# Turning x to token rows on VectorE and by copies inside the memory instead of on TensorE (attention and token mixing, one core)

## The chip, the cores and the metric

The kernel runs on one core of one Trainium2 chip. The metric is the device time of one execution in microseconds (us). A core has TensorE (PE, with its weight loads PEld), VectorE (DVE), ScalarE (ACT), GpSimd (POOL) and SyncE (SP), which here does nothing but issue DMAs. Each engine takes its instructions in the order in which the program lists them, and waits on semaphores for the others.

## The reference

Eight batches of attention (8 heads, 576 tokens, head size 64) with two kinds of masks, then a mixing block on the 512 channels that the heads make up together:

```
x = attention(q, k, v)                  # per batch: 576 tokens x 512 channels
theta = x @ w_theta
zr, zi = x * cos(theta), x * sin(theta)
y = w_tok_r @ zr + w_tok_i @ zi         # over the tokens
u = x + y
out = u + relu(u @ w_ch)
```

## The kernel before, in words

**Layout.** The attention of a batch b goes in four pairs of heads. `pv` leaves the pair's output in PSUM, `x_evac` copies it to the tile `x{pr}` in the memory: 128 rows are channels, 576 columns are tokens. theta, the residual and the channel product use x in this form (channels on the rows). The products `x * sin` and `x * cos` need the other form, tokens on the rows, since `theta` leaves theta with 128 tokens on the rows and 512 channels along them.

**Turning x.** `natural(b, st)` makes that other form for a tile `st` of 128 tokens (st 4 is the last half tile of 64): four TensorE transposes (L718) of 128 x 128 into one PSUM bank `xn`. VectorE then multiplies out of PSUM: L760 (sin, into `g`) and L702 (cos, into `K`) for tiles 0 to 3, L767 and L702 for tile 4.

**One batch's stages.** `phase(b, nb)` lists what TensorE does, and PE's order is that of the code. First come the eight *token units* `y` of batch b (L804; 27 matmuls each, over nine K tiles in the order `KORD` = 0, 4, 1, 5, 2, 6, 3, 7, 8), with the scores `s` and the products `o` of the next batches between them. The scores of pair 2 of batch b+1 stand ahead of the first token unit of batch b. Then comes the *theta stage*: theta of tile 4, 0, 1, 2, 3 of batch nb (`th`, L682 to L689), each followed by a channel unit `c` of batch b (L834, 12 matmuls) and, before the change, by the transposes of `natural`. The last three channel units end the phase.

**From theta to z.** `trig(b, st)` is a chain over ACT and DVE. ACT copies theta to an integer (`K`, L746), DVE subtracts it (L748), ACT takes the sine into `g` (L754), the absolute value (L695) and the cosine (L697), DVE multiplies both with x. `zsplit` then rounds each product on ACT (`zh{kt}`, L641) and takes the rest on POOL (`zl{kt}`, L643). Token tile st gives the K tiles st (cosine) and 4 + st (sine); tile 4 gives K tile 8. A token unit reads all of them.

**What else stands on DVE, ACT and POOL near there.** L813 takes a channel unit out of its PSUM bank (`c`, two banks `m`). The scores of a pair are masked and their row maximum taken by nine instruction pairs (L406), L495 scales the maximum, nine ACT exponentials with sums follow (L501, with a table load ahead of them after sines), DVE takes the reciprocal of the sums (L504, L505), POOL multiplies (`P`, L507), and DVE turns P by eight block transposes of 32 rows each (L522).

**What sets the order.** For the first phase (batch 0, and theta of batch 1) the order on DVE, ACT, POOL and SP comes from `Order`, a list scheduler with ranks and costs in the code. From then on only PE's order is written down; the order on the other engines is set at build time by the framework's scheduler, which simulates the program. The eight completion semaphores of SP's DMAs are used in turn, so a DMA waits until the eighth before it has landed.

Of the kernel before, what the change touches and what calls it, by code (L numbers as in the profile page):

```python
# [18 lines left out]
DM = H * D  # L19
# [40 lines left out]
class Order:  # L60
# [13 lines left out]
    def pin(self, ins):  # L74
        if self.live:
            self.tc.keep_in_program_order(ins)
# [73 lines left out]
def build(ctx, tc, qT, kT, vw, wth, wtk, wch, maskb, ident, identb, outT):  # L150
# [431 lines left out]
    def x_split(b, pr):  # L582
        yield None, ("xe", b, pr)
        x = xf[b, pr]
        yield from take(f"xh{pr}", 1, XH.get(pr) if b == 1 else None)
        hl = hp.tile([128, 2 * S], F32R, tag=f"xh{pr}", name=f"xh{b}_{pr}")
        hi = hl[:, :S]
        lo, lt = hl[:, S + 64:], hl[:, S:S + 64]
        yield "ACT", act(S)
        pin(nc.scalar.copy(hi, x))  # L590
        on = pr < 3
        eng, cost = (nc.vector, dve) if on else (nc.gpsimd, pool)
        yield "DVE" if on else "POOL", cost(64)
        pin(eng.tensor_tensor(lt, x[:, FS:], hi[:, FS:].bitcast(F32), op=ALU.subtract))
        yield "DVE" if on else "POOL", cost(FS)
        pin(eng.tensor_tensor(lo, x[:, :FS], hi[:, :FS].bitcast(F32), op=ALU.subtract))
        xh[b, pr] = hl
        signal(("xh", b, pr))

    def pv(b, pr):  # L600
        yield None, ("va", b, pr)
        yield None, ("vb", b, pr)
        yield None, ("pt", b, pr)
        if pr >= 1:
            yield None, ("pv", b, pr - 1)
# [12 lines left out]
        n = b * NP + pr  # L618
        if ra is not None:
            give("va", ra)  # L620
            go(load_va(n + 2), RANK["load"])
        if rb is not None:
            give("vb", rb)
            go(load_vb(NP if n == NP - 2 else n + 1), RANK["load"])
        if b:
            go(x_split(b, pr))

    zs = {}

# [63 lines left out]
    def cosine(b, st, f, z, kt, key, rel):  # L693
        yield "ACT", act(DM)
        pin(nc.scalar.activation(f, f, AF.Abs))  # L695
        yield "ACT", act(DM) + 90
        table(nc.scalar.activation(f, f, AF.Sin, scale=-2 * math.pi, bias=halfpi[:f.shape[0]]))  # L697
        signal(("sin", b, st))
        yield None, ("xn", b, st)
        px, rx = pxs[b, st]  # L700
        yield "DVE", dve(DM)
        pin(nc.vector.tensor_tensor(z, px, f, op=ALU.mult))  # L702
        signal(key)
        if kt is not None:
            yield None, ("px", b, st)
            give(*rx)
            yield from zsplit(b, kt, z, rel)
        elif rel:
            give(*rel)

    pxs = {}

    def natural(b, st, cs):
        px, rx = yield from bank("mmxxm"[st] if b == 0 else "x" if b == 1 else XP[st], f"xn{b}_{st}")
        px = px[:cs.stop - cs.start]
        yield "PE", 430
        for c in range(NC):
            pe(nc.tensor.transpose(px[:, 128 * c:128 * c + 128], xf[b, c][:, cs], idt))  # L718
        pxs[b, st] = px, rx
        signal(("xn", b, st))  # L720

    def trig(b, st):
        cs = slice(128 * st, min(128 * st + 128, S))
        R = cs.stop - cs.start
        yield None, ("th", b, st) if b else ("th0", st, 3)
        pt, rt = ths.pop((b, st))
        go(natural(b, st, cs))
        if b == 0 and st in FG0:
            K, gt = (hp.tile([128, DM], F32R, tag=t, name=f"{n}{b}_{st}").bitcast(F32) for t, n in zip(FG0[st], "Kg"))
            K = K.bitcast(I32)[:R]  # L730
            rf = rg = None
        else:
            rf, rg = ("f", (yield from take("f", 2))), ("g", (yield from take("g", 2)))
            K = gp.tile([128, DM], I32, tag="f", name=f"K{b}_{st}")[:R]
            gt = gp.tile([128, DM], F32, tag="g", name=f"g{b}_{st}")
        f = K.bitcast(F32)
        g = gt[:R]
        th = pt[:R]
        if R == 64 and b > 0:
            yield "ACT", act(DM)  # L740
            pin(nc.scalar.copy(g, pt[R:]))
            yield "DVE", dve(DM)
            pin(nc.vector.tensor_tensor(g, th, g, op=ALU.add))
            th = g
        yield "ACT", act(DM)
        pin(nc.scalar.activation(K, th, AF.Copy, scale=I2PI))  # L746
        yield "DVE", dve(DM)
        pin(nc.vector.scalar_tensor_tensor(out=f, in0=th, scalar=I2PI, in1=K, op0=ALU.mult, op1=ALU.subtract))  # L748
        give(*rt)
        if b == 0:  # L750
            for p in range(NP):
                yield None, ("P", 0, p)
        yield "ACT", act(DM)
        table(nc.scalar.activation(g, f, AF.Sin, scale=2 * math.pi))  # L754
        if R == 128:
            go(cosine(b, st, f, f, st, ("cos", b, st), rf))
            yield None, ("xn", b, st)
            px, rx = pxs[b, st]
            yield "DVE", dve(DM)
            pin(nc.vector.tensor_tensor(g, px, g, op=ALU.mult))  # L760
            signal(("px", b, st))
            yield from zsplit(b, 4 + st, g, rg)
        else:
            yield None, ("xn", b, st)
            px, rx = pxs[b, st]
            yield "DVE", dve(DM)
            pin(nc.vector.tensor_tensor(gt[128 - R:], px, g, op=ALU.mult))  # L767
            yield from cosine(b, st, f, g, None, ("cos", b, st), rf)
            give(*rx)
            yield from zsplit(b, 8, gt, rg)  # L770

    uh, ul = {}, {}
# [68 lines left out]
    def phase(b, nb):  # L841
        if nb >= B:
            for f, i, g in UNITS:
                go(f(b, i, g))
            return
        n = 0
        while n <= TH_AT:
            for p in S_AT:
                if S_AT[p] == n and nb + p // NP < B:
                    go(scores(nb + p // NP, p % NP))  # L850
            f, i, g = UNITS[n]
            go(f(b, i, g))
            for p in range(NP):
                if PV_AT[p] == n:
                    go(pv(nb, p))
            for p in TURN_AT:
                if TURN_AT[p] == n and nb + p // NP < B:
                    go(turn(nb + p // NP, p % NP))
            n += 1
        rest = UNITS[n:]  # L860
        for i, st in enumerate(STS):
            go(theta(nb, st))
            f, e, g = rest.pop(0)
            go(f(b, e, g))
            go(trig(nb, st))
            for p in TURN_TH:
                if TURN_TH[p] == i and nb + p // NP < B:
                    go(turn(nb + p // NP, p % NP))
        while rest:
            f, i, g = rest.pop(0)  # L870
            go(f(b, i, g))
# [55 lines left out]
    for p in range(2):  # L927
        go(scores(2, p), RANK["scores2"] + p * RANK["pair"])
        go(turn(2, p), RANK["scores2"] + p * RANK["pair"])
    go(thetas(1), RANK["theta1"])  # L930
    od.run()
    od.live = False
# [70 lines left out]
```

## Time and profile before

| | us |
|---|---|
| median of 3 runs (597.99 to 598.87) | 598.78 |
| the profiled execution's own time | 597.07 |
| its span (first to last instruction) | 595.3 |

| engine | busy us | share of the span |
|---|---|---|
| PE | 569.7 | 96% |
| DVE | 361.6 | 61% |
| ACT | 351.1 | 59% |
| POOL | 222.4 | 37% |

The phases of the batches in the middle repeat at a distance of 68.7 us. In what follows one of them is read, with times in us from the start of the span: the theta stage of batch 4 lies from 319.7 to 348.3, and the first token unit of batch 4 starts at 349.5.

### The profile page before, as it was taken

The numbers are of one execution on the slowest core, as the hardware profiler recorded it, in microseconds if no ns is written. First come the engines' busy times: TensorE is split into PE (matmuls) and PEld (weight loads), VectorE is DVE, ScalarE is ACT, GpSimd is POOL, SyncE is SP. The second block draws the span as 40 slices with busy tenths as digits, with TensorE's granted clock in tenths as the row PEclk, the third lists the DMA queues.
The fourth block names the chain that finished last, engine by engine and source line by source line (L and its number), as shares of the span: only waits on it lengthen the run. The fifth ranks groups of instructions, "written<-read, shape, count | busy, mean of one in ns | idle before, by whom it ended". The sixth has DMA issues, their size and how long they took to land.

```text
span 595.3 us, 14176 instructions
## 1 busy us (share of the span) xinstructions
PE 569.7 (96%) x5584; PEld 516.9 (87%) x5584; DVE 361.6 (61%) x1132; ACT 351.1 (59%) x939; POOL 222.4 (37%) x206
## 2 busy tenths in 40 slices
PE   5997898999999999999999999999999999999997
PEld 4744787979998899889998899989998899989997
DVE  3889888855765667465566567655665656445112
ACT  1498967687535955568553974468564785266110
POOL 2229854534322532326142442316324253315220
PEclk9999599999999999999999999999999999999999
DMA  8982347404650074302641054401742023001002
GB/s 303 398 339 61 121 160 246 142 1 141 182 160 3 2 241 142 101 2 89 197 139 62 1 181 151 154 1 40 231 142 73 0 81 100 1 1 53 28 1 81
DMA packets 26866, 67.76 MB, mean 114 GB/s; under 512 B 2992, under 2 KB 3248, under 8 KB 26800
## 3 DMA queue, kind: packets, MB, share of 16 engines
q1 hardware_dynamic: 26800, 66.86, 32.9%
q8 instruction: 44, 0.72, 0.5%
q14 instruction: 22, 0.18, 0.1%
HBM read 57.41 MB, written 9.44 MB: 112 GB/s over the span
## 4 chain that ended last, share of the span: by engine, by line
PE 49%; DVE 22%; ACT 21%; issue 3%; POOL 2%; DMA 2%; SPq 0%; ACTq 0%; DVEq 0%; POOLq 0%
PE y L804 27%; DVE pt L522 9%; PE c L834 8%; PE s L465 5%; ACT P L501 5%; PE o L614 4%; PE th L682 3%; ACT K L697 3%; ACT zh L641 3%; ACT g L754 2%; ACT K L695 2%; DVE P L406 2%; DVE K L702 2%; POOL P L507 2%; ACT L754 1%
## 5 line engine op out<-in xcount | busy, mean ns | idle before, releaser
L787 POOL TENSOR_TENSOR u<-x,u 128x288 fp32r<-128x288 f32 x64 | 54.9, 858 | 184.9 <-ACT u L785 162.2
L522 DVE STREAM_TRANSPOSE pt<-P 32x288 f32<-32x288 f32 x224 | 105.1, 469 | 21.1 <-POOL P L507 18.0
L834 PE MATMUL c<-u,late_wc 128*128 128x288 f32 x768 | 111.7, 296 | 0.8 <-DVE x L813 0.5
L834 PEld LDWEIGHTS c<-u,late_wc 128*128 128x128 f32 x768 | 106.2, 188 | 4.8 <-DVE x L813 2.0
L785 ACT CAST u<-x 128x288 fp32r<-128x288 f32 x64 | 27.5, 430 | 129.3 <-DVE x L782 129.3
L804 PE MATMUL y<-wtkh,zh 128*128 128x288 f32 x288 | 90.6, 315 | 1.1 <-ACT zh L641 1.1
L804 PE MATMUL y<-wtkh,zl 128*128 128x288 f32 x288 | 86.6, 301 | 3.7 <-POOL zl L643 3.7
L804 PE MATMUL y<-wtkl,zh 128*128 128x288 f32 x288 | 86.2, 299 | 0.0
L643 POOL TENSOR_TENSOR zl<-g,zh 128x512 fp32r<-128x512 f32 x40 | 52.6, 1316 | 79.1 <-ACT zh L641 66.7
L501 ACT ACTIVATE P<-P,mx 128x64 f32<-128x64 f32 x216 | 72.1, 336 | 16.8 <-DVE mx L495 16.8
L682 PE MATMUL th<-wthh,xh 128*128 128x512 f32 x224 | 76.3, 402 | 0.0
L782 DVE TENSOR_TENSOR x<-y,x 128x288 f32<-128x288 f32 x64 | 28.7, 450 | 66.8 <-PE y L804 64.0
L804 PE MATMUL y<-late_wt_b,zh 128*128 128x288 f32 x320 | 68.1, 297 | 0.0
L804 PE MATMUL y<-late_wt_a,zh 128*128 128x288 f32 x256 | 58.0, 308 | 2.7 <-DVE x L782 2.7
L804 PEld LDWEIGHTS y<-wtkh,zh 128*128 128x128 f32 x288 | 55.4, 192 | 4.8 <-ACT zh L641 2.3
L804 PEld LDWEIGHTS y<-wtkh,zl 128*128 128x128 f32 x288 | 55.3, 192 | 4.5 <-POOL zl L643 4.5
L804 PEld LDWEIGHTS y<-wtkl,zh 128*128 128x128 f32 x288 | 55.5, 193 | 0.3 <-issue 0.3
L643 POOL TENSOR_TENSOR zl<-K,zh 128x512 fp32r<-128x512 f32 x32 | 42.0, 1312 | 36.1 <-ACT zh L641 36.1
L507 POOL TENSOR_TENSOR P<-P,sm 128x576 f32<-128x576 f32 x32 | 37.5, 1172 | 43.8 <-ACT xh L590 19.3
L804 PEld LDWEIGHTS y<-late_wt_b,zh 128*128 128x128 f32 x320 | 51.4, 189 | 0.3
L682 PEld LDWEIGHTS th<-wthh,xh 128*128 128x128 f32 x224 | 42.1, 188 | 8.3
L804 PE MATMUL y<-late_wt_b,zl 128*128 128x288 f32 x160 | 47.3, 296 | 0.0
(103 smaller groups left out, 1110.0 us busy)
## 6 DMA issues: line engine op xcount, KB each, us to landing
q<-in_qT_dram SPq DMA_DIRECT2D x32, 576.0 KB, 4.2
va<-in_vw_dram SPq DMA_DIRECT2D x30, 320.0 KB, 3.2
out_dram<-x SPq DMA_DIRECT2D x32, 288.0 KB, 2.1
k<-in_kT_dram SPq DMA_DIRECT2D x28, 304.0 KB, 4.6
vb<-in_vw_dram SPq DMA_DIRECT2D x29, 256.0 KB, 3.4
st_wtk<-in_wtk_dram SPq DMA_DIRECT2D x8, 576.0 KB, 8.8
st_wth<-in_wth_dram SPq DMA_DIRECT2D x4, 512.0 KB, 9.8
st_wch<-in_wch_dram SPq DMA_DIRECT2D x4, 512.0 KB, 4.9
```

The lines of the kernel that those rows point to most:

```text
L465: pe(nc.tensor.matmul(ps[64 * e:64 * e + 64, n - g0], q[:, qb], k[:, QB * qb:QB * qb + BW], start=not masked, stop=not masked or n == g1 - 1))
L501: table(nc.scalar.activation(P[:, n], P[:, n], AF.Exp, bias=mx[:, n:n + 1], scale=SCALE, accum_out=sm[:, n:n + 1]))
L507: pin(nc.gpsimd.tensor_tensor(P, P, sm.unsqueeze(2).to_broadcast([128, NJ, BW]), op=ALU.mult))
L522: pin(nc.vector.transpose(pmats[b, pr][k0:k0 + QB, :, hh, QB * e:QB * e + QB], P[p0:p0 + QB, :, QB * o:QB * o + QB]))
L614: pe(nc.tensor.matmul(ps[64 * hh:64 * hh + 64, BW * j:BW * j + BW], v[:, 64 * hh:64 * hh + 64], pmats[b, pr][:, j, hh], start=True, stop=T ...
L643: pin(nc.gpsimd.tensor_tensor(lo, z, hi.bitcast(F32), op=ALU.subtract))
L682: pe(nc.tensor.matmul(pt, l, r, start=(n == 0), stop=(n == 3 * NC - 1)))
L782: pin(nc.vector.tensor_tensor(x[:, ts], ps, x[:, ts], op=ALU.add))
L785: pin(nc.scalar.copy(uh[b, d][:, ts], x[:, ts]))
L787: pin(nc.gpsimd.tensor_tensor(ul[b, d][:, ts], x[:, ts], uh[b, d][:, ts].bitcast(F32), op=ALU.subtract))
L804: pe(nc.tensor.matmul(ps, l[:, cs], r, start=(n == 0), stop=(n == 3 * NK - 1)))
L834: pe(nc.tensor.matmul(ps, l[:, cs], r[:, ts], start=(n == 0), stop=(n == 3 * NC - 1)))
```

## The change

From batch 1 on `natural` does nothing. In its place:

- `x_turn` (L726 of the changed kernel, called from `pv` behind `x_split`) turns a pair's x on VectorE: one block transpose over 128 rows x 576 columns, which turns each 32 x 32 block in itself, into the tile `xq`. Four for each batch, 28 in all.
- `x_move` (L743, called in `phase` ahead of the theta stage) brings the blocks to their rows by DMAs within the memory: each moves 32 rows x 128 words (512 B a row, 16 KB). 16 for a tile of 128 tokens, 8 for the half tile: 72 for each batch, 504 in all, all on SP. It has no tile of its own to write to: `xn` of token tile st takes the buffer of `zh{4+st}` (that of K tile 8 for the half tile). So these DMAs wait until the token units of the batch before have read that buffer for the last time, and for all four `x_turn`s; and `zh` of that K tile is written only when both products of the tile are done.
- the products (`by_x`, L765) read `xn` from the memory in place of PSUM, with the channel order of `xn` folded into the access pattern.
- `dynamic_dma_scratch_size=1024` makes room in the memory for `xq`.

Batch 0 is turned on TensorE as before.

```diff
         if b:
             go(x_split(b, pr))
+            go(x_turn(b, pr))
...
+    def x_turn(b, c):
+        yield None, ("xe", b, c)
+        if c == 0:
+            yield from take("xq", 1, b - 1)
+            xq[b] = cp.tile([128, 18, NC, QB], F32, tag="xq", name=f"xq{b}")
+        elif od.live:
+            yield None, ("got", "xq", b - 1)
+        yield "DVE", 1000
+        pin(nc.vector.transpose(xq[b][:, :, c], xf[b, c].rearrange("p (a s) -> p a s", s=QB)))
+        signal(("xq", b, c))
+
+    def x_move(b):
+        for c in range(NC):
+            yield None, ("xq", b, c)
+        if b == 1:
+            for d in range(NC):
+                yield None, ("tk", 0, d, 1)
+        for st in STS:
+            R = 64 if st == 4 else 128
+            kt = min(4 + st, 8)
+            xn = hp.tile([128, DM], F32R, tag=f"zh{kt}", name=f"xn{b}_{st}").bitcast(F32)
+            yield "DMA", dma(R // 128 * DM)
+            for a in range(R // QB):
+                for g in range(4):
+                    pin(nc.sync.dma_start(xn[QB * a:QB * a + QB, 128 * g:128 * g + 128],
+                                          xq[b][QB * g:QB * g + QB, 4 * st + a].rearrange("p a b -> p (a b)")))
+            xns[b, st] = xn[:R].rearrange("p (g c d) -> p c g d", g=4, c=NC)
+            signal(("xn", b, st))
+        give("xq", b - 1)
...
     def natural(b, st, cs):
-        px, rx = yield from bank("mmxxm"[st] if b == 0 else "x" if b == 1 else XP[st], f"xn{b}_{st}")
+        if b:
+            return
+        px, rx = yield from bank("mmxxm"[st], f"xn{b}_{st}")
...
+    def by_x(b, st, z, f):
+        if b:
+            pin(nc.vector.tensor_tensor(rows(z), xns[b, st], rows(f), op=ALU.mult))
+        else:
+            pin(nc.vector.tensor_tensor(z, pxs[b, st][0], f, op=ALU.mult))
...
             yield "DVE", dve(DM)
-            pin(nc.vector.tensor_tensor(g, px, g, op=ALU.mult))
+            by_x(b, st, g, g)
             signal(("px", b, st))
+            if b:
+                yield None, ("cos", b, st)
             yield from zsplit(b, 4 + st, g, rg)
...
         rest = UNITS[n:]
+        go(x_move(nb))
         for i, st in enumerate(STS):
             go(theta(nb, st))
...
+    go(x_move(1), 0)
     go(thetas(1), RANK["theta1"])
```

Since the scheduler of the build sets the order on DVE, ACT, POOL and SP, the order moves too. Three places around the end of the theta stage of batch 4 follow. In the names the digits behind the letter are batch and tile: `K4_3` is the cosine side of token tile 3 of batch 4, `g4_3` its sine side, `c3_3_1` the last channel unit of batch 3, `s5_2`, `P5_2`, `mx5_2`, `sm5_2` belong to the scores of pair 2 of batch 5, `y4_0_0` is the first token unit of batch 4.

**DVE, from the last channel units to the first token unit.** Before (the other L406 pairs left out):

```order
L748 SCALAR_TENSOR_TENSOR K4_3_4345<-th4_3_4312,K4_3_4345 128x512
L813 SCALAR_TENSOR_TENSOR x3_1_2844<-c3_1_1_4362,x3_1_2844 128x288
L702 TENSOR_TENSOR K4_3_4345<-xn4_3_4340,K4_3_4345 128x512
L760 TENSOR_TENSOR g4_3_4346<-xn4_3_4340,g4_3_4346 128x512
L813 SCALAR_TENSOR_TENSOR x3_3_3054<-c3_3_1_4392,x3_3_3054 128x288
L406 ISA P5_2_4407,mx5_2_4408<-s5_2_0_4410,mskb_91 128x64
L495 TENSOR_SCALAR mx5_2_4408<-mx5_2_4408 128x9
L782 TENSOR_TENSOR x4_0_3607<-y4_0_0_4456,x4_0_3607 128x288
L504 TENSOR_SCALAR sm5_2_4409<-sm5_2_4409 128x9
```

And in the changed kernel:

```order
L861 SCALAR_TENSOR_TENSOR x3_3_3172<-c3_3_1_4620,x3_3_3172 128x288
L765 TENSOR_TENSOR K4_1_4484<-xn4_1_4316,K4_1_4484 128x512
L765 TENSOR_TENSOR g4_1_4485<-xn4_1_4316,g4_1_4485 128x512
L406 ISA P5_2_4635,mx5_2_4636<-s5_2_0_4638,mskb_91 128x64
L795 SCALAR_TENSOR_TENSOR K4_3_4573<-th4_3_4545,K4_3_4573 128x512
L495 TENSOR_SCALAR mx5_2_4636<-mx5_2_4636 128x9
L504 TENSOR_SCALAR sm5_2_4637<-sm5_2_4637 128x9
L765 TENSOR_TENSOR K4_2_4528<-xn4_2_4333,K4_2_4528 128x512
L765 TENSOR_TENSOR g4_2_4529<-xn4_2_4333,g4_2_4529 128x512
L765 TENSOR_TENSOR K4_3_4573<-xn4_3_4350,K4_3_4573 128x512
L765 TENSOR_TENSOR g4_3_4574<-xn4_3_4350,g4_3_4574 128x512
L830 TENSOR_TENSOR x4_0_3778<-y4_0_0_4684,x4_0_3778 128x288
```

Before, the products of tiles 1 and 2 were long done here and those of tile 3 stood ahead of the last channel unit; now those of tile 1 stand behind the last channel unit, and those of tiles 2 and 3 behind the reciprocal of the sums of the next scores (L504, L505).

**ACT and POOL at the same place.** Before, ACT rounded the last z tiles and then took the exponentials:

```order
L697 ACTIVATE K4_3_4345<-K4_3_4345,halfpi_93 128x512
L641 CAST zh4_3_4353<-K4_3_4345 128x512
L641 CAST zh4_7_4358<-g4_3_4346 128x512
L501 ACT_TABLE_LOAD
L501 ACTIVATE P5_2_4407,sm5_2_4409<-P5_2_4407,mx5_2_4408 128x64 x9
```

Now the exponentials stand ahead of the four last z tiles:

```order
L698 ACTIVATE K4_3_4573<-K4_3_4573,halfpi_93 128x512
L501 ACT_TABLE_LOAD
L501 ACTIVATE P5_2_4635,sm5_2_4637<-P5_2_4635,mx5_2_4636 128x64 x9
L642 CAST zh4_2_4536<-K4_2_4528 128x512
L642 CAST zh4_6_4541<-g4_2_4529 128x512
L642 CAST zh4_3_4581<-K4_3_4573 128x512
L642 CAST zh4_7_4586<-g4_3_4574 128x512
```

POOL follows the same turn: its product for P5_2 (L507) stood behind all nine `zl` of batch 4, and stands now between the `zl` of K tile 5 and those of K tiles 2, 6, 3 and 7.

**SP, from the last loads of the token stage to the next ones.** Before, the outputs of batch 3 followed the loads:

```order
L220 DMA k5_3_4036<-in_kT_dram 128x608
L819 DMA out_0_dram<-x3_0_2726 128x576
L819 DMA out_0_dram<-x3_1_2844 128x576
L819 DMA out_0_dram<-x3_2_2913 128x576
L819 DMA out_0_dram<-x3_3_3054 128x576
L218 DMA q6_0_4439<-in_qT_dram 128x1152
```

In the changed kernel the 72 copies stand between:

```order
L220 DMA k5_3_4212<-in_kT_dram 128x608
L743 DMA xn4_0_4299<-xq4_3807 32x128 x4
L743 DMA xn4_4_4290<-xq4_3807 32x128 x8
L743 DMA xn4_0_4299<-xq4_3807 32x128 x12
L743 DMA xn4_1_4316<-xq4_3807 32x128 x16
L743 DMA xn4_2_4333<-xq4_3807 32x128 x16
L743 DMA xn4_3_4350<-xq4_3807 32x128 x16
L867 DMA out_0_dram<-x3_0_2840 128x576
```

The loads before them are past; the outputs and the next loads of q stand behind them.

More of the change, by code (lines that the diff above doesn't have):

```diff
@@ L699, in cosine @@
         yield None, ("xn", b, st)
-        px, rx = pxs[b, st]
         yield "DVE", dve(DM)
-        pin(nc.vector.tensor_tensor(z, px, f, op=ALU.mult))
+        by_x(b, st, z, f)
         signal(key)
         if kt is not None:
-            yield None, ("px", b, st)
-            give(*rx)
+            if not b:
+                yield None, ("px", b, st)
+                give(*pxs[b, st][1])
             yield from zsplit(b, kt, z, rel)
@@ L711, in build, with rows @@
     pxs = {}
+    xq, xns = {}, {}
+    def x_turn(b, c):
[26 more added lines that the diff above has]
+        give("xq", b - 1)
+    def rows(t):
+        return t.rearrange("p (c g d) -> p c g d", c=NC, g=4)
     def natural(b, st, cs):
-        px, rx = yield from bank("mmxxm"[st] if b == 0 else "x" if b == 1 else XP[st], f"xn{b}_{st}")
+        if b:
+            return
+        px, rx = yield from bank("mmxxm"[st], f"xn{b}_{st}")
         px = px[:cs.stop - cs.start]
@@ L757, in trig @@
             yield None, ("xn", b, st)
-            px, rx = pxs[b, st]
             yield "DVE", dve(DM)
-            pin(nc.vector.tensor_tensor(g, px, g, op=ALU.mult))
+            by_x(b, st, g, g)
             signal(("px", b, st))
+            if b:
+                yield None, ("cos", b, st)
             yield from zsplit(b, 4 + st, g, rg)
@@ L764, in trig @@
             yield None, ("xn", b, st)
-            px, rx = pxs[b, st]
             yield "DVE", dve(DM)
-            pin(nc.vector.tensor_tensor(gt[128 - R:], px, g, op=ALU.mult))
+            by_x(b, st, gt[128 - R:], g)
             yield from cosine(b, st, f, g, None, ("cos", b, st), rf)
-            give(*rx)
+            if not b:
+                give(*pxs[b, st][1])
             yield from zsplit(b, 8, gt, rg)
@@ L989 @@
     host = _arrays({n: _np.asarray(a) for n, a in inputs.items()})
-    nc = _bacc.Bacc("TRN2", target_bir_lowering=False, num_devices=1)
+    nc = _bacc.Bacc("TRN2", target_bir_lowering=False, num_devices=1,
+                     dynamic_dma_scratch_size=1024)
     arrays, args = {}, []
```

## The prediction

> **What bounds the kernel now.** I read the page first, then the busy time by stretches, then PE's waits, and last the timelines of all engines around one theta stage.
>
> ```profile
> span 595.3 us, 14176 instructions
> 276.23:344.89 68.66, 67.90 (x676) 63.06 (x676) 42.69 (x155) 42.19 (x121) 24.34 (x24) 1.00 0.32 106
> PE y L804 <- DVE x L782: 0.5, 1, 0.5
> PE c L834 <- DVE x L813: 0.2, 1, 0.2
> ```
>
> The second line is one period of the middle batches (columns: length, busy us of PE, PEld, DVE, ACT and POOL with instruction counts, PE's granted clock, DMA share, GB/s); the last two are all of PE's waits in it. PE is busy for 67.90 of 68.66 us at full clock and waits twice, 0.7 us in all. It looks like a kernel bound by PE alone, from which any PE work taken away is gain. The theta stage shows how little stands beside that:
>
> ```profile
> 319.74 0.39 PE L687 MATMUL th<-wthh,xh 128*128 128x512 f32 x1
> 323.16 0.60 PE L718 MATMUL xn<-idt,x 128*64 128x128 f32 x4
> 323.52 0.48 PE L682 MATMUL th<-wthh,xh 128*128 128x512 f32 x1
> 342.91 5.44 PE L834 MATMUL c<-u,late_wc 128*128 128x288 f32 x36
> 348.28 1.27 PE L465 MATMUL s<-k,q 128*64 128x64 f32 x36
> 349.48 0.40 PE L804 MATMUL y<-wtkh,zh 128*128 128x288 f32 x1
> ```
>
> Four transposes hold PE from 323.16 to 323.52, 0.36 us. The stage goes from 319.74 to 348.28, scores follow, and the first token unit of batch 4 starts at 349.48. At that time its last inputs are still being made:
>
> ```profile
> 348.08 1.28 POOL L643 TENSOR_TENSOR zl<-K,zh 128x512 fp32r<-128x512 f32 x1 [1.52 <-ACT zh L641]
> 349.32 1.29 POOL L643 TENSOR_TENSOR zl<-g,zh 128x512 fp32r<-128x512 f32 x1
> 353.37 0.46 DVE L782 TENSOR_TENSOR x<-y,x 128x288 f32<-128x288 f32 x1 [2.64 <-DMA q<-in_qT_dram]
> ```
>
> The `zl` of token tile 3 end at 349.3 and 350.6; PE reaches those K tiles (seventh and eighth of nine) some 2.5 and 3 us after 349.48 and never waits. The unit's end, 353.3, is seen in L782. So the z chain has about 2 us to spare there, no more: **whatever puts the products of tiles 2 and 3 later by more than that stops PE at the first token unit of every batch.**
>
> **What is removed.** 20 transposes for each of 7 batches. By the rows above 5 x 0.36 = 1.8 us of PE for a batch, 12.6 in all, at once in front of the token unit. The PSUM banks that come free cost or win nothing here: PE's two waits are on banks `m`.
>
> **What is added, and beside what it lies.**
>
> ```profile
> L522 DVE STREAM_TRANSPOSE pt<-P 32x288 f32<-32x288 f32 x224 | 105.1, 469 | 21.1 <-POOL P L507 18.0
> L760 DVE TENSOR_TENSOR g<-xn,g 128x512 f32<-128x512 f32 x32 | 21.9, 683 | 2.2 <-ACT g L754 1.3 <-PE xn L718 0.8
> L767 DVE TENSOR_TENSOR g<-xn,g 64x512 f32<-64x512 f32 x8 | 5.5, 684 | 8.9 <-ACT g L754 8.8
> 311.66 3.85 DVE L522 STREAM_TRANSPOSE pt<-P 32x288 f32<-32x288 f32 x8 [1.90 <-POOL P L507]
> ```
>
> No transpose of 128 rows is in this trace. The nearest row is L522, 469 ns for 32 rows x 288. Rows cost nothing on DVE (L767 with 64 rows and L760 with 128 take 684 and 683), so twice the columns give 0.94 us; if the four strips of 32 rows went one after another it were 3.75. I take 0.94. Three of the four lie in the token stage, where DVE is half idle (42.69 of 68.66). The fourth, of pair 3, falls into the 1.90 us in which DVE waits for P ahead of 311.66: nothing, but 2.8 us a batch at the upper end. The products read two operands from the memory instead of one from PSUM; their step (0.6, below) I leave as it is.
>
> The copies:
>
> ```profile
> 1.16 0.42 SPq L270 DMA_DIRECT2D idb<-in_identb_dram  x1
> 1.63 0.42 SPq L279 DMA_DIRECT2D q<-in_qT_dram  x1
> 280.93 0.34 SPq L218 DMA_DIRECT2D q<-in_qT_dram  x1
> 281.32 0.45 SPq L220 DMA_DIRECT2D k<-in_kT_dram  x1
> out_dram<-x SPq DMA_DIRECT2D x32, 288.0 KB, 2.1
> ```
>
> SP issues DMAs 0.39 us (280.93 to 281.32) to 0.47 us apart (1.16 to 1.63), whatever their size; a small one lands 2.1 us after. All these move 128 rows and none stays inside the memory. I take 0.39 with the 0.47 as upper row; with eight semaphores the 2.1 us allow one each 0.26 us, so issuing sets the pace. 72 of them take 28 us. All but four wait for the last token unit, which ends at 319.7; tile 1 has then landed by 319.7 + 40 x 0.39 + 2.1 = 337.4, tile 2 by 343.7, tile 3 by 349.9. Behind them in SP's queue are only outputs and a load of q for a much later pair; nobody waits for those. The buffers of `zh` bring no stall either: the casts stand behind both products anyway. The smaller scratch space touches no transfer that this kernel makes.
>
> **What is moved, and where it costs.** DVE's order in the changed kernel now has the products of tiles 2 and 3 behind L504 and L505, thus behind the nine exponentials of the next scores, which stand behind the row maxima, which need PE's scores; and the maxima stand behind the copy-out of the last channel unit and the products of tile 1. The copies may land early, DVE cannot take the products before. The links, by their rows:
>
> ```profile
> 347.26 0.68 DVE L760 TENSOR_TENSOR g<-xn,g 128x512 f32<-128x512 f32 x1
> 347.86 0.99 DVE L813 SCALAR_TENSOR_TENSOR x<-c,x 128x288 f32<-128x288 f32 x2
> 349.13 0.22 DVE L406 CUSTOM_DVE_ANT_0 P<-s,mskb 128x64 f32<-128x64 f32 x1 [0.28 <-PE s L465]
> 350.56 0.17 DVE L495 TENSOR_SCALAR mx<-mx 128x9 f32<-128x9 f32 x1
> 344.57 0.63 ACT L754 ACTIVATE g<-K 128x512 f32<-128x512 f32 x1
> 345.23 0.63 ACT L695 ACTIVATE K<-K 128x512 f32<-128x512 f32 x1
> 345.90 0.73 ACT L697 ACTIVATE K<-K,halfpi 128x512 f32<-128x512 f32 x1
> 348.62 1.28 ACT L501 ACT_TABLE_LOAD   x1
> 317.59 3.09 ACT P L501 x18
> 355.19 1.15 POOL L507 TENSOR_TENSOR P<-P,sm 128x576 f32<-128x576 f32 x1
> ```
>
> I walk them in batch 4's times. PE ends the last channel unit at 348.28 less 1.8 (transposes) less 0.2 (the wait) = 346.3. Copy-out 0.5: 346.8. Two products of tile 1, 0.6 each (347.26 to 347.86): 348.0. Five of nine maxima, 0.16 each (349.13 to 350.56): 348.8. The second half of the scores reuses the bank that these free: 16 of 36 matmuls, 0.6: 349.4. Four maxima: 350.1. The subtraction of tile 3, 0.6: 350.7. Sine, absolute value and cosine on ACT, 0.66 + 0.67 + 0.73: 352.8. Table load 1.28: 354.1. Exponentials 3.09: 357.2. Sum and reciprocal, about 0.4: 357.6. Four products: 360.0. POOL meanwhile makes P, 1.15, to 358.8, then four `zl` at 1.25 (348.08 to 349.32): 363.8. The last four matmuls of the unit: **364.3, against 353.3 now: 11.0 us late**, with PE idle for some 8 of them. From the unit's end to the next theta stage PE is full as before, so nothing takes this back: DVE's work there starts earlier against PE than it did.
>
> Batches 1 to 6 have this order (1 with small differences; there SP starts within the stage, and I hold it at 11.0 too): 66. Batch 7 has no scores behind it: the maxima, exponentials and P fall out of the chain, but tile 1's products still wait for the last channel unit, and from there copy, subtraction, two ACT steps, rounding and four `zl` follow; the same steps give about 7.5. Sum 73.5.
>
> **The clock.** A PE that idles for 8 us does not come back at full speed:
>
> ```profile
> 50.00:55.00 5.00, 3.30 (x12) 1.50 (x10) 4.52 (x8) 4.57 (x9) 4.64 (x5) 1.00 0.00 0
> 55.00:60.00 5.00, 2.60 (x27) 2.00 (x28) 4.24 (x14) 4.31 (x9) 4.57 (x4) 0.78 0.72 216
> 65.00:70.00 5.00, 4.20 (x16) 3.85 (x17) 2.88 (x6) 5.00 (x29) 4.38 (x4) 0.50 0.16 64
> 70.00:75.00 5.00, 5.00 (x35) 5.00 (x34) 4.78 (x11) 5.00 (x12) 4.99 (x5) 0.86 0.00 0
> 66.52 9.35 PE y L804 x52
> ```
>
> After waits of PE the granted clock was 0.50; dense matmuls began at 66.52, and the mean of 0.86 in the last stretch puts the return at 71.4. 4.9 us at half clock lose 2.4 us. Seven batches: 16.8; nothing if the clock held. The Trainium skill (TensorE: Matmul & The Clock Gate, Part 1: The HAM clock gate) says that PE falls to half clock after an idle window of about 3.4 us and returns after a busy one; the trace's 0.50 agrees. By its 3.4 us the loss would be 1.7 us a batch and the time 682; I stay with the trace's 2.4.
>
> **Sum.** The profiled execution took 597.07 (span 595.3, 1.8 around it), 1.7 below the median. 597.07 + 66 + 7.5 + 16.8 = **687 us**.
>
> **Rivals.**
> *The copies bound.* Tile 3's products come at 358.8 in the walk, so a pace up to (358.8 - 319.7 - 2.1) / 68 = 0.54 us hides. For it: no row shows such copies, and the dependence on eight semaphores. Against: both rows of issuing are below. At 0.70 the last products come 10.7 us later, 75 us in 7 batches: about 760. The Trainium skill (DMA: Bandwidth & Descriptors, Rules for kernel authors) speaks for this one: transfers under 64 KB are mostly overhead, and these have 16.
> *The gain that PE's share promises (the other side).* If the z of tiles 2 and 3 came before PE reaches them in the first unit, 12.6 us go: 584.5. It decides at about 2 us of delay of `zl`; DVE's order would need slack that the walk doesn't show. If instead the DVE and ACT chain of the stage, to which the wait on L813 points, takes the 1.8 us back as waiting, it stays at 597.
> *A smaller stall.* If the clock holds and the chain is 2 us shorter in each batch, 597.07 + 73.5 - 14 = 657.
>
> **How the numbers follow.** Forecast with its smaller stall 0.85, copies bound 0.10, gain 0.03, no change 0.02. The range goes from 655 (smaller stall) to 720: the forecast with DVE's 2.8 us a batch (20) and a pace a little over the threshold. Copies far above it, and the other side, are left out. About 0.2% is what a measurement tells from no change; faster 0.03, within it 0.02, slower 0.95.
>
> **What would show it.** PE's waits at the first token unit on `zh` and `zl` of K tiles 2, 6, 3, 7, 8 us or more in each batch; a period near 82; L504 ahead of the products of tiles 2 and 3 in DVE's timeline, with DVE waiting for ACT and not for DMAs; granted clock 0.5 behind each stall; L726 near 0.94. It is wrong if DVE waits for the copies at L765, or if the products come before the exponentials.

## The result, and the profile after

| | us | ratio to before |
|---|---|---|
| before, median of 4 runs (597.99 to 598.95) | 598.83 | |
| after, median of 4 runs (745.88 to 749.52) | 746.31 | 1.2478 [1.2441, 1.2515] |
| forecast 687, range 655 to 720 | | |

The kernel is slower, as forecast, by 147 us where 88 were forecast. The profiled execution took 749.52 us. Of its page the lines on the span, the chain that ended last by engine, and the copies (count, KB each, us from issue to landing):

```profile
span 747.7 us, 14680 instructions
SPq 38%; PE 24%; DVE 15%; ACT 8%; issue 6%; POOL 4%; DMA 3%; DVEq 0%; ACTq 0%; POOLq 0%
xn<-xq SPq DMA_DIRECT2D x504, 16.0 KB, 1.8
```

Of the groups by line, the cosine products of full tiles and the block transposes (count, busy us, mean ns, and the engine's idle time ahead with what ended it):

```profile
L765 DVE TENSOR_TENSOR K<-xn,K 128x512 f32<-128x512 f32 x28 | 19.3, 688 | 46.1 <-DMA xn<-xq 45.3 <-issue 0.8
L726 DVE STREAM_TRANSPOSE xq<-x 128x576 f32<-128x576 f32 x28 | 21.6, 773 | 9.0 <-ACT x L578 8.7
```

SP's queue, at 0% of this chain before, holds 38% of it, and at the cosine products of L765 DVE waits 45.3 us for the copies: the very sign that the prediction named as its refutation. One middle period by its busy times, and then all of PE's waits in it:

```profile
390.87:479.27 88.40, 70.82 (x658) 64.22 (x657) 46.31 (x159) 42.41 (x120) 24.70 (x24) 0.88 0.31 96
```

```profile
PE y L852 <- ACT zh L642: 12.9, 2, 8.1
PE s L465 <- DVE mx L406: 1.8, 1, 1.8
PE y L852 <- POOL zl L644: 1.7, 2, 1.2
PE o L614 <- ACT x L578: 0.9, 1, 0.9
```

88.4 us in place of 68.7 (82 was forecast), and PE waits for `zh` twice, not once. On `zh` and `zl` of the first token unit it waits 14.6 us in all. The timelines of SP, DVE and PE around the end of that theta stage (which begins at 393.6) show the two waits:

```profile
390.87 47.58 SPq L743 DMA_DIRECT2D xn<-xq  x72
419.77 0.69 DVE L765 TENSOR_TENSOR K<-xn,K 128x512 f32<-128x512 f32 x1
430.49 0.17 DVE L504 TENSOR_SCALAR sm<-sm 128x9 f32<-128x9 f32 x1 [6.50 <-ACT P L501]
431.07 0.69 DVE L765 TENSOR_TENSOR K<-xn,K 128x512 f32<-128x512 f32 x1 [0.16 <-issue]
431.68 1.64 DVE L765 TENSOR_TENSOR g<-xn,g 128x512 f32<-128x512 f32 x1
439.72 0.69 DVE L765 TENSOR_TENSOR K<-xn,K 128x512 f32<-128x512 f32 x1 [6.40 <-DMA xn<-xq]
432.47 0.61 PE L852 MATMUL y<-wtkh,zh 128*128 128x288 f32 x1 [8.07 <-ACT zh L642]
441.17 0.61 PE L852 MATMUL y<-wtkh,zh 128*128 128x288 f32 x1 [4.83 <-ACT zh L642]
445.11 0.46 DVE L830 TENSOR_TENSOR x<-y,x 128x288 f32<-128x288 f32 x1 [4.09 <-PE y L852]
```

The stage of batch 4 that the prediction walked began at 319.74, this one at 393.56, so its times plus 73.8 are those to compare. Up to tile 2 the walk holds to within a microsecond: both products of tile 1 done at 421.0 (walk 421.8), L504 behind the exponentials at 430.5 (walk 431.0), tile 2's products from 431.1 (walk 431.4). Then the first of tile 3's, which the walk has at 432.6, waits 6.40 us for its copies and starts at 439.7, and the unit ends at 445.1 in place of 438.1. The 72 copies held SP for 47.58 us, 0.66 us each; 0.39 was assumed.

Stage by stage, the start of the first `th<-wthl` matmul of batch 1, from there the period of each batch, and the rest, in us of the profiled executions (e1, e2, e7 and e11 are below):

| | before | after | e1 | e2 | e11 | e7 |
|---|---|---|---|---|---|---|
| start of batch 1's theta stage | 114.7 | 118.7 | 117.6 | 117.1 | 118.9 | 113.9 |
| batch 1 | 67.9 | 99.0 | 84.6 | 85.1 | 83.5 | 67.7 |
| batch 2 | 68.7 | 87.4 | 70.9 | 80.2 | 82.1 | 67.6 |
| batch 3 | 68.7 | 88.7 | 69.0 | 80.5 | 82.6 | 68.1 |
| batch 4 | 68.9 | 88.4 | 68.7 | 82.0 | 80.6 | 68.1 |
| batch 5 | 68.7 | 88.2 | 70.0 | 82.0 | 82.6 | 68.3 |
| batch 6 | 65.2 | 84.6 | 64.7 | 80.3 | 80.9 | 65.6 |
| batch 7 to the end | 72.7 | 92.8 | 70.4 | 70.5 | 80.1 | 70.4 |

The changed kernel loses 35 us with batch 1 (4.0 of them ahead of its stage), 19 to 20 with each of batches 2 to 6, and 20 with batch 7.

### The profile page after: what moved, and what is told of

It reads as the page before. It is cut to its first block, busy times and chain, and to the rows that moved or that the text cites. A ratio compares the mean times of both kernels' runs of the same rounds, so it can differ in the third digit from the quotient of the medians.

```text
span 747.7 us, 14680 instructions
## 1 busy us (share of the span) xinstructions
PE 597.8 (80%) x5444; PEld 529.5 (71%) x5444; DVE 388.6 (52%) x1160; ACT 353.9 (47%) x939; POOL 222.7 (30%) x206
## 4 chain that ended last, share of the span: by engine, by line
SPq 38%; PE 24%; DVE 15%; ACT 8%; issue 6%; POOL 4%; DMA 3%; DVEq 0%; ACTq 0%; POOLq 0%
SPq L743 38%; PE y L852 18%; DVE pt L522 6%; ACT P L501 3%; PE o L614 3%; POOL zl L644 3%; PE c L882 2%; PE s L465 2%; DMA xn<-xq 2%; DVE xq L726 1%; DVE P L406 1%; DVE xh L596 1%; DMA first_k<-in_kT_dram 1%; DMA st_wch<-in_wch_dram 1%; ACT x L578 1%
## 5 line engine op out<-in xcount | busy, mean ns | idle before, releaser
L852 PE MATMUL y<-wtkh,zh 128*128 128x288 f32 x288 | 99.7, 346 | 87.7 <-ACT zh L642 84.5
L852 PEld LDWEIGHTS y<-wtkh,zh 128*128 128x128 f32 x288 | 61.3, 213 | 95.5 <-ACT zh L642 89.8
L835 POOL TENSOR_TENSOR u<-x,u 128x288 fp32r<-128x288 f32 x64 | 51.7, 809 | 210.8 <-ACT u L833 207.3
L852 PE MATMUL y<-wtkh,zl 128*128 128x288 f32 x288 | 98.0, 340 | 17.1 <-POOL zl L644 15.3
L882 PE MATMUL c<-u,late_wc 128*128 128x288 f32 x768 | 108.8, 296 | 2.8 <-DVE x L830 2.2
L852 PE MATMUL y<-wtkl,zh 128*128 128x288 f32 x288 | 92.9, 323 | 0.0
L683 PE MATMUL th<-wthh,xh 128*128 128x512 f32 x224 | 78.5, 412 | 10.5 <-DVE K L795 10.5
L852 PEld LDWEIGHTS y<-wtkh,zl 128*128 128x128 f32 x288 | 60.8, 211 | 27.3 <-POOL zl L644 27.2
L852 PEld LDWEIGHTS y<-wtkl,zh 128*128 128x128 f32 x288 | 62.0, 215 | 0.3 <-issue 0.3
L507 POOL TENSOR_TENSOR P<-P,sm 128x576 f32<-128x576 f32 x32 | 39.8, 1245 | 75.0 <-DVE sm L505 67.2
L642 ACT CAST zh<-K 128x512 fp32r<-128x512 f32 x32 | 19.7, 615 | 74.1 <-DVE K L765 74.0
```

Of the source, the lines that this page charges most:

```text
L507: pin(nc.gpsimd.tensor_tensor(P, P, sm.unsqueeze(2).to_broadcast([128, NJ, BW]), op=ALU.mult))
L683: pe(nc.tensor.matmul(pt, l, r, start=(n == 0), stop=(n == 3 * NC - 1)))
L835: pin(nc.gpsimd.tensor_tensor(ul[b, d][:, ts], x[:, ts], uh[b, d][:, ts].bitcast(F32), op=ALU.subtract))
L852: pe(nc.tensor.matmul(ps, l[:, cs], r, start=(n == 0), stop=(n == 3 * NK - 1)))
L882: pe(nc.tensor.matmul(ps, l[:, cs], r[:, ts], start=(n == 0), stop=(n == 3 * NC - 1)))
```

## The experiments

Two causes stand in the trace, the late copies and DVE's order. The theory of the pace says that SP's issuing of 72 copies sets the time, the theory of the order (the prediction's) that the products behind L504 do. The first four runs take each with and without the other.

**e1: few transfers, and with them the old order.** x's blocks go through a scratch tensor in HBM: four writes and five reads for each batch. With these the build's scheduler puts all products ahead of L504 by itself.

```diff
+        xd = dp.tile([18, QB, 4, NC * QB], F32, tag="xd", name=f"xd{b}")
+        for g in range(4):
+            pin(nc.sync.dma_start(xd[:, :, g].rearrange("a j w -> j a w"),
+                                  xq[b][QB * g:QB * g + QB].rearrange("p a c r -> p a (c r)")))
+        xr = xd.rearrange("a j g w -> (a j) (g w)")
...
-            for a in range(R // QB):
-                for g in range(4):
-                    pin(nc.sync.dma_start(xn[QB * a:QB * a + QB, 128 * g:128 * g + 128],
-                                          xq[b][QB * g:QB * g + QB, 4 * st + a].rearrange("p a b -> p (a b)")))
+            pin(nc.sync.dma_start(xn[:R], xr[128 * st:128 * st + R]))
```

> 72 copies a batch become 4 writes of x's turned blocks into a scratch tensor in HBM and 5 reads of whole token tiles. With this few transfers the build also puts the products of tiles 2 and 3 ahead of L504 again. If copies and order are all that costs (either theory), the stall goes and what is left is the gain that PE's share promised: 597 less 12.6, about 585; between 583 and 595 if DVE's transposes or the reads cost something. If something else in the change costs (the 128-row transposes, the reads of two operands from the memory, the smaller scratch), it stays above 600.

**e2: the same transfers, the late order.** In batches 2 to 6 the products of tiles 2 and 3 (`rests`) are listed behind L505 of the next scores; what follows these products (rounding on ACT, `zl` on POOL) moves with them. `behind` fixes the order on DVE and adds no wait on another engine.

```diff
+            if (b, st) in rests:
+                behind(p, recs[b + 1, 2])
```

> As e1, but with the products of tiles 2 and 3 held behind L505 of the next scores in batches 2 to 6, as the changed kernel has them. Theory of the order (the prediction's walk): 9.8 us a batch (11.0 less the two products of tile 1, which here stay ahead of the maxima) and 2.4 us for the clock, five batches: 61 us over e1, about 646. Theory of the pace (only late copies cost): within 10 us of e1.

**e3: the 72 copies, the early order.** L504 (`add`) comes behind all products of the batch before.

```diff
+        if b > 2 and pr == 2:
+            for p in prods[b - 1]:
+                behind(add, p)
```

> The changed kernel with its 72 copies on SP, but with L504 and L505 of the next scores behind the products of tiles 2 and 3 in batches 2 to 6 (the order of the kernel before). Theory of the pace: tile 3's copies land as late as now (46 us after the stage's start), so the time stays within 10 us of 746. Theory of the order alone: the five stalls go, 5 x 12 = 60 us less, about 686.

**e4: every second copy on ACT's queue.**

```diff
-                    pin(nc.sync.dma_start(xn[QB * a:QB * a + QB, 128 * g:128 * g + 128],
+                    pin((nc.sync, nc.scalar)[g % 2].dma_start(xn[QB * a:QB * a + QB, 128 * g:128 * g + 128],
```

> The changed kernel with every second copy issued by ACT's queue instead of SP's; the build then puts tiles 2 and 3 ahead of L504 too. If issuing on one queue sets the pace, each queue has 36 x 0.63 = 23 us, the last copy lands about 25 us after the token units' end, in the stage's time, and the stall at the first token unit nearly goes: 600 to 640, with ACT's 23 us of issuing as its price. If the DMA engines set the pace, the last copy lands 46 us after, and the time is 730 to 750.

Measured (before 597.66 us, median of 7):

| | median us | ratio to before |
|---|---|---|
| e1, HBM, early order | 617.51 | 1.0342 [1.0312, 1.0373] |
| e2, HBM, late order | 679.97 | 1.1383 [1.1361, 1.1404] |
| after, 72 copies, late order | 746.31 | 1.2478 [1.2441, 1.2515] |
| e3, 72 copies, early order | 752.58 | 1.2607 [1.2570, 1.2643] |
| e4, copies on SP and ACT | 739.63 | 1.2390 [1.2355, 1.2426] |

e2 lies 62.5 us over e1, where the theory of the order had 61: with fast transfers the order alone makes a stall of the size that was forecast, with periods of 80 to 82. (The 646 of the expectation missed because it started from 585 for e1.) In e2 the sum of the exponentials, behind which the products stand, and PE's wait in the token unit:

```profile
316.21 0.17 DVE L525 TENSOR_SCALAR sm<-sm 128x9 f32<-128x9 f32 x1 [3.16 <-ACT P L522]
317.89 0.61 PE L880 MATMUL y<-wtkh,zh 128*128 128x288 f32 x1 [4.22 <-ACT zh L664]
```

But e3, in which L504 no longer stands ahead, is not faster than the changed kernel, it is 6 us slower. Its DVE waits for the copies instead (DVE's waits: us in total, times, longest):

```profile
DVE K L777 <- DMA xn<-xq: 86.6, 13, 9.1
```

So the two do not add: **the later of them sets the time, and in the changed kernel that is the copies.** e1 itself missed its 583 to 595; e6, e7 and e10 follow that up. e4's total lies in the range that was given to slow DMA engines (730 to 750), but its trace shows another reason: the copies are out sooner, and the time goes elsewhere. SP's timeline, then ACT's first step on theta and PE's theta matmuls (groups):

```profile
383.24 24.96 SPq L743 DMA_DIRECT2D xn<-xq  x36
```

```profile
L788 ACT COPY g<-th 64x512 f32<-64x512 f32 x7 | 4.1, 582 | 131.5 <-DMA xn<-xq 129.4
L683 PE MATMUL th<-wthh,xh 128*128 128x512 f32 x224 | 86.0, 448 | 80.1 <-DVE g L790 73.9
```

SP's half took 24.96 us, 0.69 each, while ACT issued the other half, so each queue issues at its own pace. But ACT's 36 copies stood in front of that step in ACT's order. ACT was idle for 131.5 us ahead of it (19 a batch), and PE's theta matmuls, which wait for the chain that begins with it, lost 80.1 us: that ate what was won.

**e11: 48 copies, the late order.** e2, with tiles 1, 2 and 3 of batches 2 to 7 brought by copies inside the memory again.

```diff
-            pin(nc.sync.dma_start(xn[:R], xr[128 * st:128 * st + R]))
+            if b == 1 or st in (4, 0):
+                pin(nc.sync.dma_start(xn[:R], xr[128 * st:128 * st + R]))
+            else:
+                for a in range(4):
+                    for g in range(4):
+                        pin(nc.sync.dma_start(xn[QB * a:QB * a + QB, 128 * g:128 * g + 128],
+                                              xq[b][QB * g:QB * g + QB, 4 * st + a].rearrange("p a b -> p (a b)")))
```

> As e2 (products of tiles 2 and 3 behind L505 in batches 2 to 6), but from batch 2 on only tiles 4 and 0 come from HBM; tiles 1, 2 and 3 come by 48 copies inside the memory on SP. At 0.65 us each the last is issued some 33 us after the stage's start and lands by 35, ahead of the 37 to 39 us at which the order lets tile 3's products go. If the later of the two sets the time, the copies hide: within 5 us of e2's 680 in batches 2 to 6, and up to 5 us more for batch 7, which has no scores to wait for: 680 to 690. If each slow copy costs whatever the order (66 us from e2 to the changed kernel over 72 copies), two thirds of it: about 724.

Measured 691.16 us, ratio 1.1530 [1.1496, 1.1563], a little over the upper end. The copies were as slow as ever (45 in a row):

```profile
369.80 29.87 SPq L774 DMA_DIRECT2D xn<-xq  x45
```

Yet batches 2 to 6 take only 3.7 us more than in e2, all five together: what lands before the order lets it be used costs next to nothing. 9.6 us come with batch 7, which has no scores behind it, so that its products wait for the copies.

**e5: what makes a copy slow to issue.** Spare copies on SP in the kernel before, into a tile `dq` that nobody reads, 16 for each shape (four for the largest).

> The kernel before, with 16 spare copies on SP at the end of each batch's token units, into a tile that nobody reads: from x in SBUF with 32 rows x 512 bytes (batch 2), 64 rows (3), 128 rows (4), four of 128 rows x 2 KB (5); from HBM with 32 rows x 512 bytes (6) and 128 rows (7). Only how long SP takes to issue each is read. If the few rows make issuing slow, 32 rows take about 0.6 us from either memory and 128 rows about 0.35. If SBUF as source makes it slow, all four shapes from SBUF take about 0.6 and both from HBM 0.33 to 0.42. Should none of them come near 0.6, it is the waiting of a copy for its source or target in the changed kernel.

One piece of SP's timeline for each shape (start, us, and how many in a row), from SBUF with 32, 64 and 128 rows of 512 bytes and 128 rows of 2 KB, then from HBM with 32 and 128 rows of 512 bytes:

```profile
151.52 3.05 SPq L847 DMA_DIRECT2D dq<-x  x5
220.93 3.02 SPq L847 DMA_DIRECT2D dq<-x  x5
289.32 3.04 SPq L847 DMA_DIRECT2D dq<-x  x5
357.80 1.20 SPq L850 DMA_DIRECT2D dq<-x  x2
365.07 3.72 SPq L853 DMA_DIRECT2D dq<-in_kT_dram  x8
381.50 1.84 SPq L853 DMA_DIRECT2D dq<-in_kT_dram  x4
```

0.60 to 0.61 us each from SBUF, whatever the rows and bytes, and 0.46 from HBM (a little over the 0.33 to 0.42 expected), for 32 rows as for 128. The pieces that are not shown scatter within one shape, from 0.56 to 0.90 from SBUF and from 0.31 to 0.79 from HBM. For a copy that ends in SBUF the source decides, not the shape; why was not tried. Where the copy ends counts too: in the changed kernel the four outputs behind the copies, from SBUF to HBM, took SP 2.06 us (from 438.55), 0.52 each. The 0.46 also says that the 0.39 between two loads in the prediction is no pace of a longer run.

**e8: batch 1 as before.** `x_turn` and `x_move` from batch 2 on; batch 1 by TensorE's transposes.

```diff
-            go(x_turn(b, pr))
+            if b > 1:
+                go(x_turn(b, pr))
...
-    go(x_move(1), 0)
```

> The changed kernel with its 72 copies, but with batch 1 turned by TensorE's transposes as before, so that the change serves batches 2 to 7. In the changed kernel's trace batch 1 cost 35 us over before (its stage began 4.0 us later and its period was 31.1 us longer), the others 19.5 to 20. If these are batch 1's own (its copies cannot start before its fourth block transpose, and its five theta tiles share one PSUM bank, which DVE frees only after the copies that it waits for), the time is 746 - 35 = 711. If batch 1 only stalls as the others do, as the prediction held, 746 - 13 to 20 = 726 to 733.

Measured 717.80 us (1.2021 [1.1977, 1.2065]): 28.5 less than the changed kernel, between the 711 and the 726 to 733 of an ordinary stall. The stages decide for the first: batch 1's period is 69.2 us in e8, against 99.0 in the changed kernel and 67.9 before, and its stage starts at 115.0, so that 33.6 of its 35 us are gone, while batches 2 to 7 together take 2.3 us more than in the changed kernel. In the changed kernel's trace the last `x_turn` of batch 1, the start of the copies, a product of tile 0 and a theta tile that waits for its PSUM bank:

```profile
120.92 0.78 DVE L726 STREAM_TRANSPOSE xq<-x 128x576 f32<-128x576 f32 x1
121.76 46.60 SPq L743 DMA_DIRECT2D xn<-xq  x72
138.43 0.69 DVE L765 TENSOR_TENSOR g<-xn,g 128x512 f32<-128x512 f32 x1 [7.69 <-DMA xn<-xq]
142.16 0.80 PE L683 MATMUL th<-wthh,xh 128*128 128x512 f32 x1 [6.72 <-DVE K L795]
```

In batch 1 all theta tiles go through the one bank `t`, which DVE's subtraction (L795) frees, and that stands behind products that wait for copies. So the lateness reaches PE in the stage itself, three times, 10.5 us in all. It is not the pace alone: with e1's nine transfers batch 1 still costs 19.6 us (2.9 ahead of its stage, 16.7 in its period). What the one bank, the late fourth block transpose and the pace each cost was not tried apart.

**e9: every second copy on POOL's queue.**

```diff
-                    pin(nc.sync.dma_start(xn[QB * a:QB * a + QB, 128 * g:128 * g + 128],
+                    pin((nc.sync, nc.gpsimd)[g % 2].dma_start(xn[QB * a:QB * a + QB, 128 * g:128 * g + 128],
```

> The changed kernel with every second copy issued by POOL's queue; the build then puts the products of tiles 2 and 3 ahead of L504. Unlike ACT in e4, POOL has 44 us a batch to spare. If one queue's issuing sets the pace, the copies land about 26 us after the token units' end and the time comes to that of e1 and POOL's issuing beside zl: 617 to 640. If the copies themselves are slow whatever issues them, it stays at 740 or more.

Measured 710.64 us (1.1894 [1.1860, 1.1929]), neither of the two. SP's, POOL's and DVE's timelines in one stage, which begins at 372.3:

```profile
369.36 23.93 SPq L743 DMA_DIRECT2D xn<-xq  x36
379.63 10.82 POOL L743 DMA_DIRECT2D xn<-xq  x22
401.60 0.69 DVE L765 TENSOR_TENSOR g<-xn,g 128x512 f32<-128x512 f32 x1 [0.42 <-issue]
```

The pace behaves as the theory says: half the copies, half SP's time, all out by 393.3. But the build gave this kernel a third order, in which the products of the second full tile begin at 401.6 only, behind the last channel unit and the next row maxima. The total says nothing of the pace.

**e6, e7 and e10: where e1's gain went.** e6 is e1 with batch 1 as before (as in e8). e7 is e6 with the units of batches 1 to 7 on three PSUM banks. e10 puts the third bank into the kernel before, whose later transposes then use bank `v` alone.

```diff
+    def unit_bank(b, name):
+        if b < 1 or od.live:
+            return bank("m", name)
+        turns[0] += 1
+        return bank("mmx"[turns[0] % 3], name)
...
-        ps, rel = yield from bank("m", f"y{b}_{d}_{g}")
+        ps, rel = yield from unit_bank(b, f"y{b}_{d}_{g}")
```

> As e1, with batch 1 turned by TensorE's transposes as before, so that DVE and the HBM way serve batches 2 to 7. In e1 batch 1's period was 84.6 us against 67.9 and its stage began 2.9 us later than before, the middle periods were equal to before (68.7 to 70). If batch 1 is all that costs, the 19.6 us go: 598. If something costs in every batch and the last ones only hid it, 603 or more.

> As e6, and from batch 1 on the token and channel units go round three PSUM banks (m, m, and x, which the transposes no longer hold) instead of two. In e1's middle batches PE had 2.2 us less to do, and waited 3.0 us for DVE's copy-outs of banks m (L865 and L834). If these waits are all that eats the gain, five or six batches gain 2 us each: 586 to 589. If DVE and ACT's chain in the stage bounds it whatever the banks, 596 to 599 as e6.

> The kernel before with its token and channel units on three PSUM banks (m, m, x), as in e7; its transposes of batches 2 to 7 then go through bank v alone. If e7's gain of 6 us comes from the third bank only, 591 to 593. If it needs the transposes off PE and out of the bank, 596 to 599, or slower where the one bank v makes PE wait for DVE's second product.

| | median us | before in the same runs | ratio |
|---|---|---|---|
| e6 | 598.74 | 597.64 | 1.0017 [1.0000, 1.0035] |
| e7 | 591.84 | 597.64 | 0.9907 [0.9886, 0.9928] |
| e10 | 631.35 | 597.51 | 1.0561 [1.0534, 1.0588] |

e6 came out as expected if batch 1 was all that cost (598). e7 lies between its two expectations (586 to 589, and 596 to 599), and e10 is the slower one that its expectation names, far over 599.

A middle period of e1, and PE's waits in it:

```profile
342.06:410.76 68.70, 65.65 (x658) 60.95 (x656) 46.54 (x158) 41.59 (x122) 25.15 (x23) 1.00 0.46 140
```

```profile
PE c L886 <- DVE x L865: 1.8, 1, 1.8
PE y L856 <- DVE x L834: 1.2, 1, 1.2
```

All of PE's waits in a middle period of e7 (249.21 to 317.31, 68.1 us):

```profile
PE c L887 <- DVE x L866: 2.1, 1, 2.1
PE y L857 <- POOL zl L646: 0.5, 1, 0.5
```

PE has 2.2 us less to do than before (65.65 against 67.9), and in e1 it waits 3.0 us for DVE to take units out of the banks `m`, at the same 68.7. The transposes' time went into waiting for DVE. Over the whole kernels, PE's matmuls behind those two copy-outs, first in e6 (two lines) and then in e7:

```profile
L857 PE MATMUL y<-late_wt_a,zh 128*128 128x288 f32 x256 | 57.5, 306 | 6.8 <-DVE x L835 6.8
L887 PE MATMUL c<-u,late_wc 128*128 128x288 f32 x768 | 113.2, 301 | 9.2 <-DVE x L866 9.2
L887 PE MATMUL c<-u,late_wc 128*128 128x288 f32 x768 | 110.2, 296 | 9.9 <-DVE x L866 9.9
```

In e7 the wait on L835 is gone, and the time is 6.9 us shorter: **e7 beats the kernel before by 0.9%.** The wait on L866, in the theta stage, is as long with three banks as with two, so the rest of the transposes' time stays there. In e1 two products stand ahead of that copy-out that take 1.10 and 0.97 us in place of 0.69 (363.05 and 364.87), which the last section comes back to; how much of the wait they make was not tried. In e10 the third bank costs more than it brings, since PE waits 29.5 us for bank `v`; in this form it is to be had only with the transposes gone.

## Why the prediction was wrong, step by step

- *What is removed* (1.8 us of PE a batch): about right, 2.2 by e1. That it counts as gain at once was wrong; e6 stands at 1.0017 with all the transposes of batches 2 to 7 gone. The rival "it stays at 597" had the place right: L813, which is L865 in e1 and L866 in e6 and e7. "The PSUM banks that come free cost or win nothing here" holds for the change as it was made; given to the units, one of them is worth 6.9 us (e7).
- *L726* (0.94 us, at no cost): 0.77. The fourth one of a batch, which stands in front of DVE's block transposes of P, is hidden in batches 2 to 6, by a hair: it ends about 0.1 us ahead of the P for which those wait (ahead of the stage walked above at 385.35, P at 385.45). In batch 1 DVE turns it at 120.92, and P was there at 117.7.
- *The order* (11.0 us a batch): right as far as tile 2's products, in the trace to a microsecond, and alone in e2, 62.5 against 61. In the changed kernel it isn't what sets the time.
- *The clock* (2.4 us a stall): too small. PE's busy time is 70.16 us in e2's period from 282.42 and 65.65 in e1's, which is 4.5 us; in the changed kernel, with two waits, 70.82, which is 5.2. The clock came back later: in e2 it stood at 0.50 for over 8 us behind the stall, in which PE had more short waits. In return PE's waits are smaller than the walk has them (10.2 us in e2's period against e1's 3.0; 6.6 of them on `zh` and `zl`, where 8 or more were named). That the 62.5 come so near to 61 is in part luck.

```profile
282.42:362.93 80.51, 70.16 (x657) 63.36 (x656) 49.88 (x158) 42.17 (x122) 25.71 (x23) 0.94 0.40 120
317.89:322.00 4.11, 2.33 (x6) 1.63 (x7) 4.11 (x3) 1.24 (x2) 4.11 (x4) 0.50 0.01 2
322.00:326.00 4.00, 3.27 (x14) 2.29 (x15) 0.22 (x2) 0.62 (x1) 2.46 (x2) 0.50 0.00 0
```

- *The copies* ("I take 0.39 with the 0.47 as upper row ... so issuing sets the pace"): **the step that failed.** Issuing does set the pace, but at 0.66 us, beyond the 0.54 up to which the walk hides them. The 0.39 is the distance of two loads from HBM; no row showed a run of copies inside the memory, and the upper end of an operation that the trace doesn't show was closed at a row of another kind. The rival "the copies bound" had the mechanism and the threshold: its own rule at 0.66 gives 687 + 7 x 68 x 0.12 = 744. That this is so near to 746 is luck: the rule has 8.2 us for every batch, where batches 2 to 6 took 6.0 each over the forecast and batch 1 took 22. It had a chance of 0.10, and the range stopped short of it. The Trainium skill spoke for it (DMA: Bandwidth & Descriptors, Rules for kernel authors: coalesce transfers under 64 KB). e1 agrees, with 9 transfers of 128 to 288 KB for 72 of 16: 617.5 us, where e3 in the same order takes 752.6.
- *Batch 1 at 11.0 and batch 7 at 7.5* (13.4 and 9.9 with the clock): 35 and 20. Of the 62 us that the profiled execution lies over the forecast, batch 1 makes 22, batches 2 to 6 make 30, batch 7 makes 10. Those of batches 2 to 6 are the pace, by e2 and e3, which fix the order there. Batch 7 points the same way: it takes 92.8 us against 70.4 in e1, but no run fixes its order. Batch 1 adds its one theta bank and its late fourth block transpose, which the walk of batch 4 doesn't have (e8).

## What to carry to other kernels

Price a row of small DMAs by a row of the same kind (source, target, queue, back to back), never by the distance of two that happen to stand together; where the trace has none, leave the upper end open in the range. Where a wait and a late order stand at the same place, the later one sets the time: mending the other alone gives nothing (e3), and a delay that fits under the order is nearly free (0.7 us a batch in e11's batches 2 to 6). Work taken off the busiest engine is gain only if the stage has nothing else at its limit; here it took a third bank as well, and even then more than half of the 2.2 us a batch went into waiting (e7).

## What the runs showed of the hardware

*Products with both operands in the memory and POOL hold each other up.* The timelines of e2 at the last products of a stage, and POOL's work beside them:

```profile
317.10 1.64 DVE L790 TENSOR_TENSOR g<-xn,g 128x512 f32<-128x512 f32 x1
318.66 1.75 DVE L790 TENSOR_TENSOR K<-xn,K 128x512 f32<-128x512 f32 x1
318.15 1.71 POOL L666 TENSOR_TENSOR zl<-K,zh 128x512 fp32r<-128x512 f32 x1
319.83 1.72 POOL L666 TENSOR_TENSOR zl<-g,zh 128x512 fp32r<-128x512 f32 x1
323.19 1.27 POOL L666 TENSOR_TENSOR zl<-g,zh 128x512 fp32r<-128x512 f32 x1
```

And in the kernel before a `zl` with a product beside it whose operand is in PSUM:

```profile
333.87 1.29 POOL L643 TENSOR_TENSOR zl<-g,zh 128x512 fp32r<-128x512 f32 x1 [10.11 <-ACT zh L641]
334.45 0.69 DVE L702 TENSOR_TENSOR K<-xn,K 128x512 f32<-128x512 f32 x1 [1.64 <-ACT K L697]
```

The same product takes 0.69 us alone and up to 1.76 beside POOL, and POOL's `zl` 1.7 in place of 1.27. In e1, 28 of the 56 products of full tiles overlap POOL by over 0.3 us and take 1.01 us in the mean, the other 28 take 0.69. In the kernel before, none of 64 takes over 0.70, the 14 beside POOL included. The prediction left this step at 0.6 us. The Trainium skill states it (SBUF — State Buffer, Who interferes with whom: a DVE instruction with two inputs in SBUF and a GpSimd one that reads SBUF shut each other out); the trace agrees. It is read from what lies beside what; no run took POOL's work away.

*Issuing.* In an unbroken run, SP issued a copy from SBUF to SBUF each 0.60 to 0.69 us (e5, the changed kernel, e4) and one from HBM to SBUF each 0.46 (e5), for 32 rows as for 128; POOL's queue issued 22 copies from SBUF to SBUF in 10.82 us, 0.49 each (e9).
